# Decode attention over long caches: 4 MB K/V tiles, weight loads in longer runs, and part of the q·k sum on TensorE

## The chip, the cores and the metric

The kernel runs on one core of one Trainium2 chip. The metric is the device time of one execution in microseconds (us); lower is better. A run with rounds executes the changed kernel six times and the kernel before eleven times on the same chip, in turn. A difference of 2% is the line between "same" and "faster" or "slower".

Engine names as in the profile: PE is TensorE (matmul), PEld its weight load, DVE is VectorE, ACT is ScalarE, POOL is GpSimd, SP is SyncE. SPq and ACTq are the sequencers of SyncE and ScalarE, from which the DMAs (loads) of this kernel are issued. Each of them takes its instructions in order: an issue that waits for a buffer holds up every later issue on that sequencer (the run split16_sync below shows it: 35.6 us).

## The reference, cut to what matters

Two independent decode steps, A and B, each with one query token, 32 heads of 128, and a cache of 16,384 rows. B looks only at the last 4,096 rows of its cache. All inputs are bf16.

```python
def _A_ref(x, k_cache, v_cache, wq, wo):        # x (1,1,512), caches (1,32,16384,128)
    q = (x @ wq).reshape(B, Sq, 32, 128).transpose(0, 2, 1, 3)
    scores = jnp.einsum("bhqd,bhkd->bhqk", q, k) * (128 ** -0.5)
    p = softmax(scores, axis=-1)
    o = jnp.einsum("bhqk,bhkd->bhqd", p, v)
    return o.transpose(0, 2, 1, 3).reshape(B, Sq, 32 * 128) @ wo
# _B_ref: the same with k_cache[:, :, Sk - W:, :], v_cache[:, :, Sk - W:, :], W = 4096
# result: concatenate([A, B], axis=-1)
```

Every byte of the caches is used once: 268.4 MB of K and V for A, 67.1 MB for B, 16.8 MB of weights, 352.3 MB in all. The work per byte is small, so this is a problem of loading.

## The kernel before

For each head, K is loaded with 128 partitions of consecutive rows. The score of a row is a multiply on VectorE and a sum over 128 columns, done as a tree of adds on VectorE; the softmax is taken without subtracting a maximum; P·V is one small matmul per row of a partition, accumulated in PSUM. A's head is two units of 64 rows per partition (2 MB of K and 2 MB of V each), B's head is one unit of 32 rows.

```python
    for u in range(NU):                        # A: 2 units of U=64; B: 1 unit of U=32
        kt = kt_pool.tile([P, U, DH], BF16, tag="kt")              # 3 buffers of 2 MB
        nc.sync.dma_start(out=kt[:, :, :], in_=kh[:, u * U : (u + 1) * U, :])
        vt = vt_pool.tile([P, U, DH], BF16, tag="vt")              # 3 buffers of 2 MB
        nc.scalar.dma_start(out=vt[:, :, :], in_=vh[:, u * U : (u + 1) * U, :])
        ...                                    # cut: a GpSimd share that is 0 here
        nc.vector.tensor_tensor(out=prod[...], in0=kt[...], in1=q_broadcast, op=ALU.mult)
        src, width = prod[:, :, :], DH
        while width > 8:                       # 128 -> 64 -> 32 -> 16 -> 8
            dst = tree_pool.tile([P, U, width // 2], BF16, ...)
            nc.vector.tensor_tensor(out=dst, in0=src[left], in1=src[right], op=ALU.add)
            src, width = dst, width // 2
        nc.vector.tensor_reduce(out=sc[:, :], in_=src, axis=X, op=ALU.add)
        nc.scalar.activation(out=p_sb, in_=sc, func=Exp, scale=..., accum_out=colsum)
        for c in range(U):
            nc.tensor.matmul(o_ps[0:1, :], lhsT=p_sb[:, c : c + 1], rhs=vt[:, c, :], ...)
        nc.tensor.matmul(s_ps, lhsT=colsum, rhs=ones_col, ...)
    ...                                        # cut: divide, transpose, multiply by wo
```

K is on the sync queue and V on the scalar queue here already. The weights come in pieces: wq in eight blocks of 512 columns and wo in four blocks of eight heads, for each problem. Each partition's part of such a load consists of runs of 1 KB. q is computed as one row of 512, copied, and spread over 128 partitions by a second matmul.

The softmax here doesn't subtract the row's maximum and nothing guards it: scores larger than these inputs give would overflow.

Of the kernel before, what the change touches and what calls it, by code (L numbers as in the profile page):

```python
# [10 lines left out]
P = 128  # L12
ACT = mybir.ActivationFunctionType
ALU = mybir.AluOpType

HQ, DH = 32, 128


class _ProblemState:
# [3 lines left out]
def _setup_init(nc, st, *, singles):  # L23
    x, wq, wo = st.x, st.wq, st.wo
    D = wq.shape[0]
    st.KC = D // P
    st.NBLK = (HQ * DH) // 512
    xT = singles.tile([P, st.KC], BF16, tag=f"xT{st.name}")
    for c in range(st.KC):
        st.dq.dma_start(  # L30
            out=xT[:, c : c + 1],
            in_=x[0, 0:1, c * P : (c + 1) * P].rearrange("a b -> b a"),
        )
    st.xT = xT
    st.qrow = singles.tile([1, HQ * DH], BF16, tag=f"qrow{st.name}")
    st.qall = singles.tile([P, HQ, DH], BF16, tag=f"qall{st.name}")
    st.wo_view = wo.rearrange("(h p) f -> p h f", p=P)
    st.WOC = 8


def _setup_block(nc, st, j, *, wqb_pool, psq_pool, ones_row):
    KC = st.KC
    wqb = wqb_pool.tile([P, KC, 512], BF16, tag="wqb")
    st.dq.dma_start(
        out=wqb[:, :, :],
        in_=st.wq[:, j * 512 : (j + 1) * 512].rearrange("(c p) f -> p c f", p=P),
    )
    qr_ps = psq_pool.tile([1, 512], F32, tag="qr")
    for kc in range(KC):
        nc.tensor.matmul(  # L50
            qr_ps[0:1, :],
            lhsT=st.xT[:, kc : kc + 1],
            rhs=wqb[:, kc, :],
            start=(kc == 0),
            stop=(kc == KC - 1),
        )
    nc.scalar.copy(st.qrow[0:1, j * 512 : (j + 1) * 512], qr_ps[0:1, :])  # L57
    qbc_ps = psq_pool.tile([P, 4, DH], F32, tag="qbc")
    nc.tensor.matmul(  # L59
        qbc_ps[:, :, :],  # L60
        lhsT=ones_row[0:1, :],
        rhs=st.qrow[0:1, 4 * j * DH : (4 * j + 4) * DH],
        start=True,
        stop=True,
    )
    nc.scalar.copy(st.qall[:, 4 * j : 4 * j + 4, :], qbc_ps[:, :, :])  # L66


def _head(
    nc,  # L70
    st,
    h,
    *,
    small,
    kt_pool,
    vt_pool,
    prod_pool,
    tree_pool,
    wo_pool,
    pso_pool,  # L80
    pss_pool,
    pst_pool,
    ident11,
    ones_col,
):
    U, NU, W = st.U, st.NU, st.W
    inv_sqrt_dh = 1.0 / math.sqrt(DH)

    o_ps = pso_pool.tile([1, DH], F32, tag="o")
    s_ps = pss_pool.tile([1, 1], F32, tag="S")  # L90
    kh = st.k_view[h].rearrange("(p l) d -> p l d", p=P)
    vh = st.v_view[h].rearrange("(p l) d -> p l d", p=P)
    for u in range(NU):
        kt = kt_pool.tile([P, U, DH], BF16, tag="kt")
        nc.sync.dma_start(out=kt[:, :, :], in_=kh[:, u * U : (u + 1) * U, :])
        vt = vt_pool.tile([P, U, DH], BF16, tag="vt")
        nc.scalar.dma_start(out=vt[:, :, :], in_=vh[:, u * U : (u + 1) * U, :])  # L97

        prod = prod_pool.tile([P, U, DH], BF16, tag="prod")
        G = st.G  # L100
        if G > 0:
            nc.gpsimd.tensor_tensor(
                out=prod[:, 0:G, :],
                in0=kt[:, 0:G, :],
                in1=st.qall[:, h : h + 1, :].broadcast_to([P, G, DH]),
                op=ALU.mult,
            )
        nc.vector.tensor_tensor(  # L108
            out=prod[:, G:U, :],
            in0=kt[:, G:U, :],  # L110
            in1=st.qall[:, h : h + 1, :].broadcast_to([P, U - G, DH]),
            op=ALU.mult,
        )
        sc = small.tile([P, U], F32, tag="scores")
        src = prod[:, :, :]
        width = DH
        RT = 8
        while width > RT:
            half = width // 2
            dst = tree_pool.tile([P, U, half], BF16, tag=f"tree{half}")  # L120
            nc.vector.tensor_tensor(  # L121
                out=dst[:, :, :],
                in0=src[:, :, 0:half],
                in1=src[:, :, half:width],
                op=ALU.add,
            )
            src, width = dst[:, :, :], half
        nc.vector.tensor_reduce(  # L128
            out=sc[:, :],
            in_=src,  # L130
            axis=mybir.AxisListType.X,
            op=ALU.add,
        )
        p_sb = small.tile([P, U], BF16, tag="p")
        colsum = small.tile([P, 1], F32, tag="colsum")
        nc.scalar.activation(  # L136
            out=p_sb[:, :],
            in_=sc[:, :],
            func=ACT.Exp,
            scale=inv_sqrt_dh,  # L140
            accum_out=colsum[:, 0:1],
        )
        for c in range(U):
            nc.tensor.matmul(  # L144
                o_ps[0:1, :],
                lhsT=p_sb[:, c : c + 1],
                rhs=vt[:, c, :],
                start=(u == 0 and c == 0),
                stop=(u == NU - 1 and c == U - 1),
            )  # L150
# [155 lines left out]
```

## Time and profile before

Three runs given at first: 863.2, 864.6 and 869.43 us, median 864.6.

| what | before | where it is read |
|---|---|---|
| HBM read | 352.32 MB, 407 GB/s over the span | the page, DMA part |
| load rate from 100 to 800 us | 414 to 424 GB/s | table of stretches |
| VectorE busy | 754.1 us (87%) | the page, busy times |
| TensorE busy | 470.9 us (54%) | the page, busy times |
| packets of 16 KB, 8 KB, 1 KB | 16,427 of 621 ns, 8,210 of 316 ns, 16,384 of 49 ns | packet records of the trace |

These lines of the page of the kernel before give busy times per engine, then rows of 40 slices of the span (each digit is the busy share in tenths; the last row is GB/s).

```profile
span 864.7 us, 12580 instructions
PE 470.9 (54%) x5520; PEld 414.9 (48%) x5520; DVE 754.1 (87%) x707; ACT 73.8 (9%) x291; POOL 0.2 (0%) x4
...
DVE  2699888969898499999989779999999759999995
...
DMA  8999999999999999999999999999999999999992
GB/s 324 413 402 415 415 425 416 421 419 420 420 416 405 426 402 425 418 427 425 425 427 415 416 425 424 416 428 424 426 425 424 409 426 392 403 423 428 426 424 93
```

The DMA row is at 9 nearly everywhere: the kernel is bound by its loads. VectorE is a busy second. Next are the costliest groups of instructions of the same kernel: line, engine, operation, output<-input, count, then busy us and mean ns of one, then the engine's idle time before them and what ended it.

```profile
L108 DVE TENSOR_TENSOR prod<-kt,qall 128x8192 bf16<-128x8192 bf16 (+1 forms) x96 | 355.0, 3698 | 37.9 <-DMA kt<-in_A_k_cache_dram 30.1
L121 DVE TENSOR_TENSOR dst<-dst 128x1024 bf16<-128x1024 bf16 (+3 forms) x288 | 185.9, 657 | 0.1
L121 DVE TENSOR_TENSOR dst<-prod 128x4096 bf16<-128x4096 bf16 (+1 forms) x96 | 184.2, 1918 | 0.0
L128 DVE TENSOR_REDUCE sc<-dst 128x64 f32<-128x512 bf16 (+1 forms) x96 | 55.8, 581 | 0.1
```

The adds of the second line (186 us) are what the change takes off VectorE and gives to TensorE; a reduce like that of the fourth line stays. The table of stretches has, for each, its length, the busy us (and instruction count) of PE, PEld, DVE, ACT and POOL, then the granted TensorE clock, the DMA share and GB/s. These lines are from two such tables of the kernel before:

```profile
100.00:200.00 100.00, 58.34 (x637) 48.61 (x636) 83.66 (x77) 10.82 (x37) 0.00 (x0) 0.73 1.01 419
...
400.00:500.00 100.00, 49.24 (x586) 44.70 (x586) 90.64 (x87) 6.95 (x32) 0.00 (x0) 0.76 1.01 422
...
840.00:848.00 8.00, 0.37 (x3) 0.19 (x3) 8.00 (x9) 0.78 (x3) 0.00 (x0) 0.62 0.67 281
```

In the middle the DMA engines are full. Only at the end (840 to 848 us) are they not, with VectorE busy without a break. There only V's last load is missing. These lines of the timeline are from the end (start us, length us, engine and line, operation, and in brackets how long the engine had stood idle and what released it):

```profile
837.85 1.95 PE L144 MATMUL o_ps<-vt,p_sb 128*1 128x128 bf16 x32 [0.76 <-ACT p_sb L136]
...
847.93 0.26 ACT L136 ACTIVATE p_sb<-sc 128x64 bf16<-128x64 f32 x1 [3.90 <-DVE sc L128]
847.94 0.34 ACTq L97 DMA_DIRECT2D vt<-in_B_v_cache_dram  x1
```

### The profile page before, as it was taken

How to read it: one execution, taken by the hardware profiler on the slowest of the kernel's cores; microseconds unless marked ns; L12 is line 12 of the kernel's file. 1: busy time of each engine (PE TensorE's matmuls, PEld its weight loads, DVE VectorE, ACT ScalarE, POOL GpSimd, SP SyncE). 2: the span in 40 equal slices, each digit the busy share in tenths (PEclk: the TensorE clock that was granted, in tenths of full speed). 3: DMA queues.
4: the chain of work that ended last, by engine and by line, in shares of the span. 5: the costliest groups of instructions: out<-in, count | busy, mean ns of one | idle time of the engine just before them, and what ended most of it. 6: DMA issues, size and time to landing. Idle time of an engine off the chain costs nothing.

```text
span 864.7 us, 12580 instructions
## 1 busy us (share of the span) xinstructions
PE 470.9 (54%) x5520; PEld 414.9 (48%) x5520; DVE 754.1 (87%) x707; ACT 73.8 (9%) x291; POOL 0.2 (0%) x4
## 2 busy tenths in 40 slices
PE   1166764675745364645655256656555345554766
PEld 0055653465634353645655256555555334454665
DVE  2699888969898499999989779999999759999995
ACT  1001111111110011000000000000000000000001
POOL 0000000000000000000000000000000000000000
PEclk9987767768678676788878687687768667687777
DMA  8999999999999999999999999999999999999992
GB/s 324 413 402 415 415 425 416 421 419 420 420 416 405 426 402 425 418 427 425 425 427 415 416 425 424 416 428 424 426 425 424 409 426 392 403 423 428 426 424 93
DMA packets 45625, 353.14 MB, mean 408 GB/s; under 512 B 4609, under 2 KB 20993, under 8 KB 20994
## 3 DMA queue, kind: packets, MB, share of 16 engines
q10 hardware_dynamic: 22784, 176.17, 49.2%
q1 hardware_dynamic: 22786, 176.17, 49.0%
q8 instruction: 43, 0.70, 0.3%
q14 instruction: 12, 0.10, 0.0%
HBM read 352.32 MB, written 0.00 MB: 407 GB/s over the span
## 4 chain that ended last, share of the span: by engine, by line
DVE 44%; DMA 31%; PE 15%; issue 9%; ACTq 0%; ACT 0%; DVEq 0%
DMA vt<-in_A_v_cache_dram 25%; DVE prod L108 24%; DVE dst L121 15%; PE o_ps L144 14%; DVE sc L128 4%; DMA kt<-in_B_k_cache_dram 3%; DMA vt<-in_B_v_cache_dram 2%; PE out_ps L175 1%; DVE ocol L170 0%; DVE recip L159 0%; DMA xT<-in_B_x_dram 0%; ACTq L97 0%; PE ocol_ps L168 0%; ACT orow L161 0%; ACT final_sb L274 0%
## 5 line engine op out<-in xcount | busy, mean ns | idle before, releaser
L144 PE MATMUL o_ps<-vt,p_sb 128*1 128x128 bf16 x5120 | 412.1, 256 | 220.3 <-ACT p_sb L136 130.8
L144 PEld LDWEIGHTS <-p_sb 128*1 128x1 bf16 x5120 | 389.0, 101 | 248.3 <-ACT p_sb L136 185.7
L108 DVE TENSOR_TENSOR prod<-kt,qall 128x8192 bf16<-128x8192 bf16 (+1 forms) x96 | 355.0, 3698 | 37.9 <-DMA kt<-in_A_k_cache_dram 30.1
L121 DVE TENSOR_TENSOR dst<-dst 128x1024 bf16<-128x1024 bf16 (+3 forms) x288 | 185.9, 657 | 0.1
L121 DVE TENSOR_TENSOR dst<-prod 128x4096 bf16<-128x4096 bf16 (+1 forms) x96 | 184.2, 1918 | 0.0
L175 PE MATMUL out_ps<-woc,ocol 128*1 128x512 bf16 x64 | 31.5, 492 | 89.0 <-DVE ocol L170 67.0
L136 ACT ACTIVATE p_sb<-sc 128x64 bf16<-128x64 f32 (+1 forms) x96 | 23.7, 247 | 426.1 <-DVE sc L128 422.5
L128 DVE TENSOR_REDUCE sc<-dst 128x64 f32<-128x512 bf16 (+1 forms) x96 | 55.8, 581 | 0.1
L161 ACT ACTIVATE orow<-o_ps,recip 1x128 bf16<-1x128 f32 x64 | 22.9, 358 | 332.2 <-DVE recip L159 332.2
L159 DVE RECIPROCAL recip<-s_ps 1x1 f32<-1x1 f32 x64 | 9.6, 150 | 47.8 <-PE s_ps L151 47.7
L175 PEld LDWEIGHTS <-ocol 128*1 128x1 bf16 x64 | 5.3, 83 | 85.3 <-DVE ocol L170 78.1
L50 PE MATMUL qr_ps<-wqb,xT 128*1 128x512 bf16 x64 | 20.4, 443 | 27.5 <-DMA wqb<-in_B_wq_dram 15.2
L151 PE MATMUL s_ps<-ones_col,colsum 128*1 128x1 f32 x192 | 18.7, 167 | 28.5 <-DVE recip L159 28.5
L151 PEld LDWEIGHTS s_ps<-ones_col,colsum 128*1 128x1 f32 x192 | 13.7, 87 | 32.4 <-DVE recip L159 31.6
L170 DVE COPY ocol<-ocol_ps 128x1 bf16<-128x1 bf16 x64 | 9.4, 147 | 20.9 <-PE ocol_ps L168 20.9
L168 PEld LDWEIGHTS <-orow 1*128 1x128 bf16 x64 | 6.0, 94 | 40.7 <-ACT orow L161 30.1
L168 PE MATMUL ocol_ps<-ident_94,orow 1*128 1x1 bf16 x64 | 11.2, 175 | 24.5 <-ACT orow L161 24.3
L50 PEld LDWEIGHTS <-xT 128*1 128x1 bf16 x64 | 4.8, 87 | 37.5 <-issue 31.0
L136 ACT ACTIVATION_READ_ACCUMULATOR p_sb<-sc 128x1 f32 x96 | 17.9, 186 | 0.0
L57 ACT CAST qrow<-qr_ps 1x512 bf16<-1x512 f32 x16 | 9.1, 571 | 23.4 <-PE qr_ps L50 23.4
L66 ACT CAST qall<-qbc_ps 128x512 bf16<-128x512 f32 x16 | 9.1, 571 | 1.5 <-PE qbc_ps L59 1.3
L59 PE MATMUL qbc_ps<-qrow,ones_row 1*128 1x512 bf16 x16 | 7.2, 450 | 1.3 <-ACT qrow L57 1.3
(11 smaller groups left out, 4.6 us busy)
## 6 DMA issues: line engine op xcount, KB each, us to landing
vt<-in_A_v_cache_dram ACTq DMA_DIRECT2D x64, 2048.0 KB, 15.9
kt<-in_A_k_cache_dram SPq DMA_DIRECT2D x64, 2048.0 KB, 15.5
kt<-in_B_k_cache_dram SPq DMA_DIRECT2D x32, 1024.0 KB, 14.1
vt<-in_B_v_cache_dram ACTq DMA_DIRECT2D x32, 1024.0 KB, 13.8
wqb<-in_A_wq_dram SPq DMA_DIRECT2D x8, 512.0 KB, 19.1
woc<-in_A_wo_dram SPq DMA_DIRECT2D x4, 1024.0 KB, 22.7
wqb<-in_B_wq_dram ACTq DMA_DIRECT2D x8, 512.0 KB, 22.8
woc<-in_B_wo_dram ACTq DMA_DIRECT2D x4, 1024.0 KB, 24.6
```

The lines of the kernel that those rows point to most:

```text
L50: nc.tensor.matmul(qr_ps[0:1, :], lhsT=st.xT[:, kc : kc + 1], rhs=wqb[:, kc, :], start=(kc == 0), stop=(kc == KC - 1),)
L108: nc.vector.tensor_tensor(out=prod[:, G:U, :], in0=kt[:, G:U, :], in1=st.qall[:, h : h + 1, :].broadcast_to([P, U - G, DH]), op=ALU.mult,)
L121: nc.vector.tensor_tensor(out=dst[:, :, :], in0=src[:, :, 0:half], in1=src[:, :, half:width], op=ALU.add,)
L128: nc.vector.tensor_reduce(out=sc[:, :], in_=src, axis=mybir.AxisListType.X, op=ALU.add,)
L136: nc.scalar.activation(out=p_sb[:, :], in_=sc[:, :], func=ACT.Exp, scale=inv_sqrt_dh, accum_out=colsum[:, 0:1],)
L144: nc.tensor.matmul(o_ps[0:1, :], lhsT=p_sb[:, c : c + 1], rhs=vt[:, c, :], start=(u == 0 and c == 0), stop=(u == NU - 1 and c == U - 1),)
L151: nc.tensor.matmul(s_ps[0:1, 0:1], lhsT=colsum[:, 0:1], rhs=ones_col[:, 0:1], start=(u == 0), stop=(u == NU - 1),)
L159: nc.vector.reciprocal(recip[:, :], s_ps[0:1, 0:1])
L161: nc.scalar.activation(out=orow[:, :], in_=o_ps[0:1, :], func=ACT.Copy, scale=recip[0:1, 0:1],)
L168: nc.tensor.transpose(ocol_ps, orow, ident11)
L170: nc.vector.tensor_copy(ocol[:, :], ocol_ps[:, :])
L175: nc.tensor.matmul(st.out_ps[0:1, :], lhsT=ocol[:, 0:1], rhs=st.woc[:, h % WOC, :], start=(h == 0), stop=(h == HQ - 1),)
```

## The change

The intent is fewer and longer runs for the DMA engines, and less work for VectorE:

- A's K and V are loaded as whole heads: 4 MB tiles, 32 KB runs, two buffers each instead of three of 2 MB.
- B is done in groups of four heads: one 4 MB tile, filled by four 1 MB loads of 8 KB runs.
- wq comes in one load of 4 MB with 32 KB runs (it borrows a V buffer), wo in runs of 4 KB.
- After the multiply and one add on VectorE, eight accumulating matmuls with the identity add the remaining 64 columns to 8 in PSUM, and one VectorE reduce of PSUM finishes the sum.
- x arrives in one DMA, and q is made on all 128 partitions at once, by a matmul with x broadcast over the columns of the stationary operand.
- Smaller parts: B's weights come from the sync queue instead of ScalarE's, the product of the multiply has one buffer instead of two (VectorE alone writes and reads it), and the output rows of four heads are gathered before wo is applied.

```diff
-    for u in range(NU):
-        kt = kt_pool.tile([P, U, DH], BF16, tag="kt")
-        nc.sync.dma_start(out=kt[:, :, :], in_=kh[:, u * U : (u + 1) * U, :])
-        vt = vt_pool.tile([P, U, DH], BF16, tag="vt")
-        nc.scalar.dma_start(out=vt[:, :, :], in_=vh[:, u * U : (u + 1) * U, :])
+    kt = cx.kt_pool.tile([P, L, DH], BF16, tag="kt", name="kt")          # L = 128, whole head
+    nc.sync.dma_start(out=kt[:, :, :], in_=st.k_view[h].rearrange("(p l) d -> p l d", p=P))
+    vt = cx.vt_pool.tile([P, L, DH], BF16, tag="vt", name="vt")
+    nc.scalar.dma_start(out=vt[:, :, :], in_=st.v_view[h].rearrange("(p l) d -> p l d", p=P))
+    for u in range(L // U):
+        p_sb, cs = _scores(nc, cx, kt[:, u * U : (u + 1) * U, :], None, [(0, U, q)])
+        _pv(...)                                                         # 64 matmuls, as before
...                                                  # _scores, after the multiply:
-        while width > RT:
-            dst = tree_pool.tile([P, U, half], BF16, tag=f"tree{half}")
-            nc.vector.tensor_tensor(out=dst, in0=src[left], in1=src[right], op=ALU.add)
-        nc.vector.tensor_reduce(out=sc[:, :], in_=src, axis=X, op=ALU.add)
+    nc.vector.tensor_tensor(out=half, in0=prod[:, :, 0:64], in1=prod[:, :, 64:128], op=ALU.add)
+    red = cx.red_pool.tile([P, U, 8], F32, tag="red", name="red")        # PSUM
+    for b in range(8):
+        nc.tensor.matmul(red, lhsT=cx.ident, rhs=half[:, :, b * 8 : (b + 1) * 8],
+                         start=(b == 0), stop=(b == 7))
+    nc.vector.tensor_reduce(out=sc[:, :], in_=red[:, :, :], axis=AX.X, op=ALU.add)
...
-    wqb_pool, wo blocks of (p h f) order, qrow and qbc matmuls            # 1 KB runs
+    wq_t = cx.vt_pool.tile([P, KC, N], BF16, tag="vt", name="wq_t")
+    nc.sync.dma_start(out=wq_t, in_=st.wq.rearrange("(p c) f -> p c f", c=KC))
+    nc.sync.dma_start(out=st.wo_t, in_=st.wo[8 heads].rearrange("(g p j) f -> p g (j f)", g=2, j=4))
+    nc.tensor.matmul(q_ps[:, :], lhsT=xb[:, c, :], rhs=wq_t[:, c, 512 columns], ...)
...
-    kt_pool = tile_pool(name="kt", bufs=3);  vt_pool = tile_pool(name="vt", bufs=3)
+    cx.kt_pool = pool("kt", 2);  cx.vt_pool = pool("vt", 2)              # of 4 MB each
...
     for h in range(32):
+        if h == G - 1: _weights_q(nc, cx, stB)                           # G = 4
+        _head_A(nc, cx, stA, h)
+        if h % G == G - 1: _group_B(nc, cx, stB, h - G + 1)
-        _head(nc, stA, h);  _head(nc, stB, h)
```

(Several lines are shortened to their core; a "..." marks a cut.)

## The prediction

> **What bounds the kernel now.** The loads. The page shows 352.3 MB read from HBM in 864.7 us (407 GB/s), the DMA row at 9 in nearly every slice, and the two load queues at 98% of the 16 engines' time. The table of stretches gives 414 to 424 GB/s from 100 to 800 us. VectorE is second (754 us, 87%). The chain of waits names VectorE for 44%, DMA for 31%, but those are buffers coming free: a faster VectorE would find the same full DMA engines.
>
> From the packet records: 16,427 packets of 16 KB took 621 ns each, 8,210 of 8 KB 316 ns, 16,384 of 1 KB (all weights) 49 ns: about 10 ns per packet plus 38 per KB. Stretches with K/V alone mostly run at 424 to 429 GB/s, those where a quarter of the bytes are weights near 400. The Trainium skill ("DMA: Bandwidth & Descriptors", Where 436 GB/s comes from) puts the ceiling at 435 GB/s; the best stretches are within 2% of it. 352.3 MB at 435 would be 810 us, an estimated floor.
>
> **What changes.**
> - DMA, on the critical path: 32 KB runs for A's K/V (8,192 packets at an estimated 1,232 ns) save about 5 us; weights in 4 and 32 KB runs (estimated 649 instead of 803 us summed over 16 engines) about 10. B's K/V stays at 8 KB.
> - Start: x in one DMA instead of four, and wq no longer behind it: 2 us earlier. B's wq needs a V buffer and may hold up the sync queue at head 3 for a few us.
> - VectorE, off the path: per 64-row unit it keeps the multiply (4.41 us) and first add (2.27) and swaps the rest (1.2+0.67+0.41+0.67) for one PSUM reduce, estimated at 0.7. 80 units: about 600 us, down from 754.
> - TensorE, off the path: 640 matmuls of 128x512 at 0.22 to 0.44 us, 140 to 280 us more.
> - Buffers: two of 4 MB each instead of three of 2. By durations K is held 13 us, V 25 us after landing, out of 39 us for two heads; K can run ahead of V, so both queues should rarely be empty.
> - Tail: the last loads were starved of buffers from 840 us (245 GB/s to 850), then 12 us of work followed. Afterwards the last group needs 9 us if V lands last, about 20 if K does: perhaps 2 to 7 us worse.
>
> **Sum.** 864.6 - 15 (packets) - 2 (start) - 4 (starved end) + 4 (tail, wq gap) is about 847; I take **846 us**, range **829 to 862** (8 in 10). Faster by over 2% **0.50**, within 2% **0.47**, slower by over 2% **0.03**. Most of the large saving on VectorE should not show.
>
> **What would show it.** Right: no 1 KB packets; 426 to 431 GB/s in the middle; VectorE near 600 us and waiting for K loads; TensorE busier by 140 to 280 us; 10 to 20 us of work after the last load. Wrong: middle stretches under 415 GB/s with both queues waiting for buffers; VectorE waiting long on TensorE's sums.
>
> **What would make it wrong.** Two large buffers may leave both queues empty once per head (slower); TensorE's order may make the next scores wait for V. On the other side, longer runs may get closer to 435 GB/s than fitted, and steadier supply may remove the stretches at 373 to 408 GB/s (faster, to 829).

## The result, and the profile after

| | before | after |
|---|---|---|
| median us, four runs each | 866.08 (863.2 to 869.43) | 856.73 (855.16 to 861.37) |
| ratio, 95% interval | | 0.9888 (0.984 to 0.9935) |

A ratio here, and below, is the mean time of one kernel's runs over the mean of the other's runs of the same rounds, so it is not quite the ratio of the medians that are quoted. The gain is 1.1% and lies within 2%: "same". The prediction had said 846 us, a gain of 2.2%, with "faster by over 2%" as the slightly likelier class. The time lies in its range, which was 33 us wide; about half of the gain that it forecast arrived (9.4 us between the medians, where 864.6 to 846 would be 18.6).

These are the lines of the page after that answer to those shown above.

```profile
span 855.4 us, 13729 instructions
PE 565.1 (66%) x6335; PEld 425.1 (50%) x6336; DVE 590.3 (69%) x346; ACT 64.7 (8%) x275; POOL 0.7 (0%) x6
...
DVE  0469775975783866947967397656969378785791
...
DMA  9999999999999899999999999999999999999992
GB/s 392 423 424 379 420 432 432 426 426 427 434 422 435 334 431 439 424 429 419 433 421 437 423 425 431 427 429 409 419 429 427 434 421 428 432 427 430 401 398 87
```

Two slices stand out against their neighbours at 420 to 439 GB/s: 379 (the fourth, 64 to 86 us) and 334 (the fourteenth, 278 to 299 us). (A packet is counted in the slice where it starts, so that single slices scatter by some GB/s.) Next come the groups after:

```profile
L73 DVE TENSOR_TENSOR prod<-kt,qallA 128x8192 bf16<-128x8192 bf16 x64 | 282.9, 4420 | 90.4 <-DMA kt<-in_A_k_cache_dram 89.5
L90 PE MATMUL red<-half,ident 128*128 128x512 bf16 x640 | 169.0, 403 | 84.5 <-DVE half L80 84.4
L80 DVE TENSOR_TENSOR half<-prod 128x4096 bf16<-128x4096 bf16 x80 | 182.6, 2283 | 0.6
...
L98 DVE TENSOR_REDUCE sc<-red 128x64 f32<-128x512 f32 x80 | 54.1, 680 | 37.0 <-PE red L90 35.6
```

VectorE fell from 754 to 590 us, nearly the 600 that had been forecast, and now waits 89.5 us for K. The Trainium skill ("VectorE: DVE Perf Modes", the perf-mode tier table) gives tensor_reduce one speed for all types, and the traces agree: the reduce of 512 float32 columns of PSUM took 680 ns here, that of 512 bf16 columns of SBUF 668 ns in the run after_tree below. The stretches after:

```profile
100.00:200.00 100.00, 71.91 (x801) 53.16 (x800) 72.11 (x42) 11.40 (x40) 0.00 (x0) 0.88 1.00 427
200.00:300.00 100.00, 62.50 (x684) 45.55 (x683) 71.77 (x40) 5.79 (x29) 0.00 (x0) 0.80 0.97 409
300.00:400.00 100.00, 70.03 (x818) 55.04 (x816) 69.44 (x41) 6.50 (x32) 0.00 (x0) 0.88 1.01 431
```

The rate rose to 427 and 431 GB/s, but from 200 to 300 us it is 409, lower than before (417), at a DMA share of 0.97.

Where did the time go? The trace records each DMA packet with its start, length, size and queue. From these records I split the span of a profiled run into four parts that sum to it: from the start to the first packet of K, V or weights; the time in which such a packet was in flight, summed over the 16 DMA engines and divided by 16 (busy); the engine time without one between the first and the last load packet, likewise divided by 16 (idle); and from the end of the last load packet to the end of the span (tail).

| us | span | start | busy | idle | tail |
|---|---|---|---|---|---|
| before | 864.7 | 4.3 | 838.6 | 9.4 | 12.4 |
| after | 855.4 | 1.8 | 824.9 | 14.4 | 14.3 |
| difference | -9.3 | -2.5 | -13.7 | +5.0 | +1.9 |

The start and the busy time fell about as forecast (-2 and -15). But the loads now stand idle for 5 us more, and the tail is 2 us longer. Each row is one profiled run. A second profile of the changed kernel (after_again, below) has busy 825.9, idle 14.2 and tail 16.0; so a difference of 1 us in busy time or of 2 us in the tail can be chance. The forecast had put these two at zero together (-4 for the starved end, +4 for tail and wq).

Much of the idle time lies in a few places. I looked for stretches with fewer than 11 of the 16 engines loading. Before, there is one of weight, at the end (845.0 to 849.6 us, 3.6 us lost), the "starved end" of the prediction, and a small one at 722.6 (0.7). After, that one has gone, and two new ones are in the middle: 66.0 to 68.5 (2.2 us lost) and 286.2 to 291.5 (3.7); three smaller ones (593, 795, 826 us) lose 1.8 together. One more is at the very end, 838.3 to 841.0 (2.4): all loads had been issued by then, and from 839 to 841 a single packet was in flight at a time, where it is 16 when all engines load. This is the timeline of the kernel after around the larger one: start, length, engine, instruction, and in brackets how long the engine had stood idle and what released it.

```profile
263.78 0.26 ACT L102 ACTIVATE p_sb<-sc 128x64 bf16<-128x64 f32 x1 [0.60 <-DVE sc L98]
...
278.09 4.43 DVE L73 TENSOR_TENSOR prod<-kt,qallA 128x8192 bf16<-128x8192 bf16 x1 [14.29 <-DMA kt<-in_A_k_cache_dram]
282.43 0.68 DVE L98 TENSOR_REDUCE sc<-red 128x64 f32<-128x512 f32 x1
...
285.35 4.42 DVE L73 TENSOR_TENSOR prod<-kt,qallA 128x8192 bf16<-128x8192 bf16 x1
285.37 2.29 PE L90 MATMUL red<-half,ident 128*128 128x512 bf16 x5 [20.01 <-DVE half L80]
...
287.82 2.93 PE L117 MATMUL o_ps<-vt,p_sb 128*1 128x128 bf16 x26
...
289.80 0.33 SPq L195 DMA_DIRECT2D kt<-in_B_k_cache_dram  x1
...
297.71 0.33 ACTq L177 DMA_DIRECT2D vt<-in_A_v_cache_dram  x1
```

The chain of waits of the same kernel, taken of the stretch from 250 to 300 us alone, starts with the load that all of this waits for (start, length, what):

```profile
245.85 32.15 DMA kt<-in_A_k_cache_dram
```

Read it as a ring. VectorE and TensorE each take their instructions in order.

1. The next head's K was issued at 245.85 and, sharing the DMA engines with V and wo, took 32.15 us until all 4 MB had landed.
2. VectorE waited for it 14.29 us. Behind this wait, in its program, stood the last step of the current head's scores: the reduce at 282.43, whose matmuls had ended by 265.4 (TensorE's 20.01 us of idle time before 285.37 say when).
3. The current head's first unit was ready for P·V even then, for ScalarE had made its probabilities at 263.78. But TensorE's program has the sum for the next head's first unit ahead of it, and so it stood idle for 20.01 us until VectorE's add of that unit was done.
4. P·V of both units ran only from 287.82, without a wait for V on its part. V's buffer came free at its end, and the next V was issued at 297.71.
5. The next head's K buffer came free when its second multiply ended (285.35 + 4.42), and the next K load was issued at 289.80.

So the loads that had been issued ran out: by the packet records about 11 engines were at work at 286.2 and none at 289.5. At 66 us it was alike: the next V load was issued at 67.34, the next K load at 67.69, each when its buffer came free.

### The profile page after: what moved, and what is told of

The parts are those of the page before. It is cut to its first block, busy times and chain, and to the rows that moved or that the text cites. A ratio compares the mean times of both kernels' runs of the same rounds, so it can differ in the third digit from the quotient of the medians. Undisturbed runs are those within 1.5% of the kernel's fastest.

```text
span 855.4 us, 13729 instructions
## 1 busy us (share of the span) xinstructions
PE 565.1 (66%) x6335; PEld 425.1 (50%) x6336; DVE 590.3 (69%) x346; ACT 64.7 (8%) x275; POOL 0.7 (0%) x6
## 4 chain that ended last, share of the span: by engine, by line
DMA 55%; DVE 21%; PE 15%; issue 7%; another core or an unknown queue 1%; ACT 1%; ACTq 0%; SPq 0%; DVEq 0%
DMA kt<-in_A_k_cache_dram 26%; DMA vt<-in_A_v_cache_dram 16%; DVE prod L73 12%; PE o_ps L117 10%; DVE half L80 6%; DMA kt<-in_B_k_cache_dram 6%; DMA xTB<-in_B_x_dram 4%; PE red L90 3%; DMA vt<-in_B_v_cache_dram 3%; DVE sc L98 3%; ACT orow L139 0%; PE oc_ps L144 0%; DVE recip L137 0%; PE outB L156 0%
## 5 line engine op out<-in xcount | busy, mean ns | idle before, releaser
L117 PE MATMUL o_ps<-vt,p_sb 128*1 128x128 bf16 x5120 | 351.9, 236 | 112.2 <-DMA vt<-in_A_v_cache_dram 82.6
L117 PEld LDWEIGHTS <-p_sb 128*1 128x1 bf16 x5120 | 333.9, 92 | 132.8 <-issue 112.1
L73 DVE TENSOR_TENSOR prod<-kt,qallA 128x8192 bf16<-128x8192 bf16 x64 | 282.9, 4420 | 90.4 <-DMA kt<-in_A_k_cache_dram 89.5
L90 PE MATMUL red<-half,ident 128*128 128x512 bf16 x640 | 169.0, 403 | 84.5 <-DVE half L80 84.4
L80 DVE TENSOR_TENSOR half<-prod 128x4096 bf16<-128x4096 bf16 x80 | 182.6, 2283 | 0.6
L90 PEld LDWEIGHTS <-ident 128*128 128x128 bf16 x640 | 58.8, 101 | 124.5 <-issue 69.7
L73 DVE TENSOR_TENSOR prod<-kt,qallB 128x4096 bf16<-128x4096 bf16 x32 | 72.0, 2284 | 11.1 <-DMA kt<-in_B_k_cache_dram 9.4
L98 DVE TENSOR_REDUCE sc<-red 128x64 f32<-128x512 f32 x80 | 54.1, 680 | 37.0 <-PE red L90 35.6
L144 PEld LDWEIGHTS <-orow 1*32 1x32 bf16 x256 | 12.2, 111 | 103.6 <-ACT orow L139 60.1
L144 PE MATMUL oc_ps<-one,orow 1*32 1x1 bf16 x256 | 17.4, 171 | 54.1 <-ACT orow L139 53.7
L124 PE MATMUL s_ps<-ones_col,cs 128*1 128x1 f32 x192 | 18.3, 165 | 18.2 <-DVE recip L137 17.6
L124 PEld LDWEIGHTS s_ps<-ones_col,cs 128*1 128x1 f32 x192 | 11.4, 84 | 31.5 <-DVE recip L137 19.7
L156 PE MATMUL outA<-wo_t,oc 128*1 128x512 bf16 x32 | 12.3, 528 | 4.9 <-DVE oc L153 4.9
L45 PEld LDWEIGHTS <-xbA 128*128 128x128 bf16 x32 | 3.7, 116 | 18.6 <-DVE xbA L40 13.6
## 6 DMA issues: line engine op xcount, KB each, us to landing
wo_t<-in_A_wo_dram SPq DMA_DIRECT2D x4, 1024.0 KB, 21.2
```

Source lines behind the costliest of these rows:

```text
L45: nc.tensor.matmul(q_ps[:, :], lhsT=xb[:, c, :], rhs=wq_t[:, c, j * 512 : (j + 1) * 512], start=(c == 0), stop=(c == KC - 1),)
L73: nc.vector.tensor_tensor(out=prod[:, k0 : k0 + n, :], in0=kv[:, k0 : k0 + n, :], in1=q.rearrange("p (o d) -> p o d", o=1).broadcast_to([P ...
L80: nc.vector.tensor_tensor(out=half[:, :, :], in0=prod[:, :, 0 : DH // 2], in1=prod[:, :, DH // 2 : DH], op=ALU.add,)
L90: nc.tensor.matmul(red[:, :, :], lhsT=cx.ident[:, :], rhs=half[:, :, b * W : (b + 1) * W], start=(b == 0), stop=(b == nb - 1),)
L98: nc.vector.tensor_reduce(out=sc[:, :], in_=red[:, :, :], axis=AX.X, op=ALU.add)
L124: nc.tensor.matmul(s_ps[0:1, 0:1], lhsT=cs, rhs=cx.ones_col[:, 0:1], start=first, stop=last,)
```

## The experiments

In the 18 kernels below, "after" stands for the changed kernel and "split16" for the first repair of it. The expectations name some theories by a letter; where a letter is not spelled out there, it stands for what follows. P: long runs make the packets cheaper, and this is what the change gains. L: it matters that a tile of 4 MB lands and comes free as a whole, so that the engines wait for the second half before they may start on the first. G: the size of a buffer is what counts, two of 4 MB against four of 2 MB. K and V: one of the two loads alone makes the gaps. T: the sum on TensorE costs time at the end. S: the slack that it gives VectorE is needed once the tiles are large. E: the order of the last groups makes the tail. R: VectorE is held up by small steps that wait for TensorE (reciprocal, row cast). Q: TensorE's program order makes the tail. I: V's loads are held up because ScalarE issues them between its other work.

All outputs are right. This table has all results; the last four columns are the split of the profiled run, as above. Most were profiled within 1.6 us of their median; after_tree 3.4 us above it (its slowest execution), split16_sync 2.2 us below, split16_tree_free 10 us below.

| run | median us | ratio to before (95%) | start | busy | idle | tail |
|---|---|---|---|---|---|---|
| after_again | 859.04 | 0.9896 (0.9852 to 0.9940) | 1.8 | 825.9 | 14.2 | 16.0 |
| split16 | 855.02 | 0.9845 (0.9806 to 0.9885) | 1.9 | 828.6 | 7.1 | 15.5 |
| tiles2mb | 860.54 | 0.9912 (0.9875 to 0.9948) | 1.8 | 827.9 | 7.9 | 20.7 |
| w1k | 868.85 | 1.0004 (0.9967 to 1.0041) | 2.2 | 833.7 | 17.2 | 14.9 |
| splitk | 858.36 | 0.9899 (0.9869 to 0.9929) | 1.8 | 826.5 | 10.0 | 17.3 |
| splitv | 855.54 | 0.9861 (0.9827 to 0.9894) | 2.0 | 826.4 | 9.3 | 16.4 |
| wqfirst | 855.21 | 0.9863 (0.9834 to 0.9893) | 1.8 | 824.6 | 11.9 | 15.6 |
| before_pesum | 874.27 | 1.0085 (1.0053 to 1.0117) | 4.4 | 837.9 | 9.8 | 19.0 |
| after_tree | 857.00 | 0.9903 (0.9872 to 0.9934) | 1.8 | 826.1 | 19.2 | 11.6 |
| split16_tree | 861.48 | 0.9950 (0.9920 to 0.9980) | 1.8 | 828.6 | 10.5 | 18.3 |
| alast | 857.50 | 0.9900 (0.9870 to 0.9930) | 1.8 | 828.3 | 8.1 | 18.7 |
| alast_tree | 862.05 | 0.9949 (0.9916 to 0.9981) | 1.8 | 828.4 | 10.5 | 21.2 |
| after_free | 860.18 | 0.9917 (0.9883 to 0.9950) | 1.8 | 827.2 | 13.9 | 15.1 |
| split16_free | 857.29 | 0.9887 (0.9849 to 0.9925) | 1.9 | 830.3 | 7.0 | 16.7 |
| split16_tree_free | 870.24 | 1.0010 (0.9964 to 1.0056) | 1.8 | 831.5 | 9.0 | 16.2 |
| alast_tree_free | 873.73 | 1.0067 (1.0032 to 1.0102) | 1.8 | 831.8 | 27.4 | 11.4 |
| split16_sync | 890.66 | 1.0266 (1.0223 to 1.0308) | 2.0 | 833.6 | 24.5 | 26.8 |
| split16_ahead | 855.54 | 0.9857 (0.9826 to 0.9888) | 1.8 | 827.8 | 7.9 | 15.5 |

### First call: packets or landing? (after_again, split16, tiles2mb, w1k)

after_again is the changed kernel once more, without an edit, as the yardstick.

> The changed kernel, unaltered, as the control of this call. About 857 us (855 to 861), 0.985 to 0.993 of the kernel before. Theory G (buffers): the idle of the 16 DMA engines between the first and the last load comes to 6 to 9 us again, at nearly the same places (near 66 and 286 us), because the order of each engine's instructions is fixed. Theory N (noise): the gaps lie elsewhere or are gone.

It measured 859.04 us (855.68 to 864.17), with gaps at the same places: 66.2 us (2.5 lost), 286.9 (2.6) and 796 to 800 (2.1). So the gaps belong to the program and not to one run.

split16 keeps everything of the change but loads A's tiles in two halves. A unit can start when its half has landed; the runs are 16 KB again. The buffers stay two of 4 MB.

```diff
-    nc.sync.dma_start(out=kt[:, :, :], in_=st.k_view[h].rearrange("(p l) d -> p l d", p=P))
-    nc.scalar.dma_start(out=vt[:, :, :], in_=st.v_view[h].rearrange("(p l) d -> p l d", p=P))
+    for u in range(L // U):
+        nc.sync.dma_start(out=kt[:, u * U : (u + 1) * U, :], in_=kh[:, u * U : (u + 1) * U, :])
+        nc.scalar.dma_start(out=vt[:, u * U : (u + 1) * U, :], in_=vh[:, u * U : (u + 1) * U, :])
```

> A's 4 MB K and V tiles are filled by two DMAs of 2 MB each, so 16 KB runs as before the change; buffers and everything else as after. Theory P (time of the packets adds up on the 16 engines): 16,384 packets at 621 ns instead of 8,192 at 1,224 ns are 157 us of engine time, 10 us slower than after, about 867 us. Theory L (landing): the first half of a tile can be worked on 5 to 10 us earlier, K buffers come free earlier, the gaps near 286 us and some of the tail go: at most 3 us slower than after, or faster.

It measured 855.02 us; all six runs (854.61 to 855.48) lie below the fastest of after_again (855.68). Busy time rose by 2.7 us, idle time fell by 7.1. So the long runs of A's K and V save about 3 us of packet time, and landing as a whole costs more than that. The stretches around the gap show it, first in the kernel after, then in split16 (the last two numbers are DMA share and GB/s):

```profile
276.00:284.00 8.00, 0.00 (x0) 0.00 (x0) 5.91 (x3) 0.35 (x2) 0.00 (x0) 0.50 1.01 434
284.00:292.00 8.00, 6.63 (x48) 4.16 (x48) 7.97 (x4) 0.00 (x0) 0.00 (x0) 0.55 0.47 179
292.00:300.00 8.00, 7.94 (x144) 7.74 (x141) 4.53 (x2) 0.36 (x1) 0.00 (x0) 1.00 1.02 421
```

```profile
276.00:284.00 8.00, 5.51 (x22) 2.17 (x23) 5.00 (x4) 0.36 (x1) 0.00 (x0) 0.79 1.00 419
284.00:292.00 8.00, 3.42 (x9) 1.01 (x7) 5.23 (x4) 0.70 (x4) 0.00 (x0) 0.79 1.02 431
292.00:300.00 8.00, 7.49 (x131) 7.17 (x130) 3.55 (x1) 0.00 (x0) 0.00 (x0) 1.00 0.99 418
```

In split16 no gap is left before 829 us; one at 829.5 to 834.1 loses 2.3 (see the fifth call). VectorE's longest wait for a K of A falls from 14.3 to 9.6 us.

tiles2mb makes the buffers themselves small: A's tiles are 2 MB again (four buffers of K, four of V), B goes in pairs of heads, and wq takes two buffers. Everything else is the change.

```diff
+        kt = cx.kt_pool.tile([P, U, DH], BF16, tag="kt", name="kt")       # in the loop over units
+        nc.sync.dma_start(out=kt[:, :, :], in_=kh[:, u * U : (u + 1) * U, :])
-    cx.kt_pool = pool("kt", 2)
-    cx.vt_pool = pool("vt", 2)
+    cx.kt_pool = pool("kt", 4)
+    cx.vt_pool = pool("vt", 4)
```

> Four K and four V buffers of 2 MB instead of two of 4 MB, the same bytes of SBUF; 16 KB runs for A's K/V and wq. Theory G (the idle DMA time after the change comes from giving back buffers 4 MB at a time): idle between first and last load falls from 8 to under 3 us and the tail after the last load from 15.5 to about 12 us, so 8 to 9 us faster than split16, within 3 us of after. Rival (gaps come from the order of TensorE's work or from wq of B, whatever the tile size): within 3 us of split16, gaps as in after.

The idle time fell to 7.9 us, about as in split16, so giving buffers back in halves adds nothing to landing in halves. But the tail grew to 20.7 us, and the time is 860.54, no better than after_again and 5.5 us slower than split16. Theory G had the fall of the idle time about right (6.3 us against after_again), but split16 has it too with 4 MB buffers; the time was missed because of the tail, and why the tail grew is not shown.

w1k keeps the change but brings the weights in runs of 1 KB again (wq in eight column blocks, wo in four).

```diff
-    nc.sync.dma_start(out=wq_t[:, :, :], in_=st.wq.rearrange("(p c) f -> p c f", c=KC))
+    for j in range(N // 512):
+        nc.sync.dma_start(out=wq_t[:, :, j * 512 : (j + 1) * 512], in_=wq_v[:, :, j * 512 : (j + 1) * 512])
```

> The changed kernel with its weights alone in 1 KB runs again (same tiles, same buffers, one DMA per 512 columns). Theory P: 16,384 packets at 49 ns instead of 256 at 1,224 and 2,048 at 162 ns are 159 us of engine time: 10 us slower than after, about 867 us. Rival (the weights' short runs cost little, the gain of the change came from elsewhere): within 3 us of after.

It measured 868.85 us, 9.8 us above after_again: the whole gain of the change has gone. Its 16,386 packets of 1 KB (two of them are the stores of the result) took 49.9 ns each. Busy time rose by 7.8 us, idle by 3.0. The weights, a twentieth of the bytes, account for about the whole net gain of the change.

### Second call: which load, wq, and the sum alone (splitk, splitv, wqfirst, before_pesum)

splitk loads only K in halves, splitv only V.

```diff
-    nc.sync.dma_start(out=kt[:, :, :], in_=...)          # splitk; splitv: the scalar line of vt
+    for u in range(L // U):
+        nc.sync.dma_start(out=kt[:, u * U : (u + 1) * U, :], in_=kh[:, u * U : (u + 1) * U, :])
```

> The changed kernel with only A's K tiles filled by two DMAs of 2 MB (16 KB runs); V whole. Theory K (the gaps come from K: scores of a head can start only when all 4 MB of K have landed, the K buffer comes back late, and TensorE, which has the next head's score sums ahead of this head's P.V in its program, gives V back late too): the gaps in the middle go as in split16, under 1.5 us in all, about 855 us. Rival V (whole V tiles are what holds up the queues): gaps of 5 us or more stay, about 859 us.

> The changed kernel with only A's V tiles filled by two DMAs of 2 MB; K whole. Theory K: gaps of 5 us or more stay near 66 and 286 us, 858 to 861 us. Rival V: gaps go, about 855 us.

Neither came out as a theory of K alone or V alone had it. The gap at 66 has gone in both, and that at 286 is 0.6 us or nothing; but each has a late gap, splitk 3.4 us at 819 to 826, splitv 3.4 at 789 to 796. Only with both halves is the middle free of gaps. By time splitv (855.54) is as good as split16, splitk (858.36) is not. Their profiled runs differ by less (spans 854.0 and 855.6), and this is idle time (9.3 and 10.0) and tail (16.4 and 17.3); the rest of the 2.8 us between the medians stays open.

wqfirst loads B's wq at the start instead of at head 3, to see whether the gap at 66 us comes from wq holding a V buffer.

```diff
     _weights_q(nc, cx, stA)
+    _weights_q(nc, cx, stB)
     for h in range(stA.H):
-        if h == G - 1:
-            _weights_q(nc, cx, stB)
```

> The changed kernel with B's wq and q worked out at the very start, before A's head 0. Theory W (the gap at 66 us is B's wq waiting for a V buffer and holding up the sync queue): that gap of 2.2 to 2.5 us goes and the time falls by about as much, to 856 us or so; the gap near 286 us stays. Rival: the gap at 66 us is the first K buffers coming back late (head 0's scores start only at 34 us) and stays, or moves, with no gain over 1 us.

The gap at 66 did not go: it moved to 75.8 to 78.5 and kept its size (2.4 us). That at 286 went, others came (387 us, 1.0 lost; 791 us, 2.5 lost). The time, 855.21, was 3.8 us below after_again, though that was another chip. By ratio (0.9863 against 0.9896, and 0.9845 for split16) the intervals overlap; moving one load may thus be worth nearly as much as the halves, and why is not shown. So the place of a gap depends on where in the sequence the wq load stands, but the wq load is not its cause; the prediction's "wq gap" was not what lies at 66 us.

before_pesum is the kernel before with only the sum changed: one add on VectorE, eight identity matmuls, one PSUM reduce.

```diff
-        while width > RT:                     # tree of four adds on VectorE
-            ...
+        nc.vector.tensor_tensor(out=half, in0=prod[:, :, 0:64], in1=prod[:, :, 64:128], op=ALU.add)
+        red = st.red_pool.tile([P, U, WR], F32, ...)                     # PSUM
+        for b in range(nb):
+            nc.tensor.matmul(red, lhsT=st.ident, rhs=half[:, :, b * WR : (b + 1) * WR], ...)
```

> The kernel before with one part of the change alone: after the first add, 512 elements per 64 rows are summed on TensorE (8 identity matmuls, 4 for B) and one reduce from PSUM; loads, tiles and weights as before. Theory D (the loads bound it, VectorE's time is off the path): VectorE busy falls from 754 to about 600 us and the time changes by less than 4 us (862 to 868), the most it can win being the 3.6 us of DMA idle at 845 us. Rival (the chain of waits, with 44% VectorE, is to be believed): faster by 10 us or more.

VectorE's busy time fell to 607.9 us, and the kernel became 0.85% slower: 874.27 us, all six runs (872.93 to 876.02) above the kernel before's highest of this call (871.45). Busy and idle time of the loads did not move; the tail grew from 12.4 to 19.0 us. The timeline of its end shows one reason. (Here the sum also shares the two PSUM buffers of q's projection; the profile names 12.3 us of waits of q's matmuls for the reduce, and no run separates these.)

```profile
851.88 4.15 PE L149 MATMUL o_ps<-vt,p_sb 128*1 128x128 bf16 x59
855.87 0.19 PE L156 MATMUL s_ps<-ones_col,colsum 128*1 128x1 f32 x2
855.99 1.68 PE L126 MATMUL red<-half,ident 128*128 128x512 bf16 x7
857.78 0.69 DVE L133 TENSOR_REDUCE sc<-red 128x64 f32<-128x512 f32 x1 [6.55 <-PE red L126]
```

The score sum of a late unit stands in TensorE's queue behind the P·V of the unit before it (851.88 to 855.99), and VectorE waits 6.55 us. On VectorE the same sum waited for nobody.

### Third call: is VectorE's relief needed at all? (after_tree, split16_tree, alast, alast_tree)

after_tree is the change with the sum back on VectorE; split16_tree is the same on split16.

```diff
-    half = cx.half_pool.tile(...); nc.vector.tensor_tensor(out=half, ...)
-    for b in range(nb): nc.tensor.matmul(red, lhsT=cx.ident, rhs=half[...], ...)
-    nc.vector.tensor_reduce(out=sc[:, :], in_=red[:, :, :], axis=AX.X, op=ALU.add)
+    while width > 8:
+        nc.vector.tensor_tensor(out=dst, in0=src[:, :, 0:hw], in1=src[:, :, hw:width], op=ALU.add)
+    nc.vector.tensor_reduce(out=sc[:, :], in_=src, axis=AX.X, op=ALU.add)
```

> The changed kernel with the sum on VectorE as before the change (adds down to 8 columns, one reduce), TensorE's identity matmuls gone. Theory T (the sum on TensorE costs at the end: the last scores wait there behind the P.V matmuls of the head before): tail after the last load from 15.5 to about 12 us, time about 855 us, 3 to 4 us faster than after. Rival S (with 4 MB tiles VectorE's slack is needed to give K buffers back in time): VectorE busy near 755 us, more idle DMA time in the middle, slower than after by 3 us or more.

> split16 (A's 4 MB tiles filled in two halves) with the sum on VectorE. Theory T: tail from 14.4 to about 11 us and no new gaps, since the halves land early enough: about 852 us, 3 us faster than split16. Rival S: slower than split16 by 3 us or more, gaps of several us back.

In after_tree both theories show and cancel: the tail is 11.6 us, shorter by 4.4 than after_again's, and the idle time 19.2, longer by 5.0. The time is the same (ratios 0.9903 and 0.9896). The split is of after_tree's slowest execution, so its sizes are rough. On split16 the relief is worth 6.5 us (861.48 against 855.02, on the same chip; ratios 0.9950 and 0.9845): with the tree the idle time rises by 3.4 us and the tail by 2.8. That the tail rose too, where in after_tree it fell, was against T.

alast (built on split16) puts B's last group before A's last four heads, so that the end is one head and not four.

```diff
-        if h % G == G - 1:
+        if h % G == G - 1 and h < stA.H - 1:
+        if h == stA.H - G - 1:
+            _group_B(nc, cx, stB, stA.H - G)
+            _store(nc, cx, stB, out, stA.DN)
```

> split16 with B's last group worked before A's last four heads, so that the last loads are the halves of one A head instead of four B heads. Theory E (the tail is the last group's serial end: four heads' P.V and finish after the last load, 2.4 us each): tail from 14.4 to 8 or 10 us, about 850 us. Rival: the tail is the last scores' path through VectorE and TensorE, whatever the heads, and stays above 13 us; no gain.

> alast with the sum on VectorE. If T and E both hold and add: tail 7 to 8 us, about 848 us, 2% under the kernel before. If only E holds: as alast. If S holds: slower than alast.

E was a miss: the tail grew, from 15.5 to 18.7 us (alast against split16) and to 21.2 with the tree. In alast the last reduce of scores waits 7.68 us for TensorE's sum, which stands behind P·V. These two have a flaw as well: the store of B's row is now issued on the sync queue ahead of A's last K loads. It cost little here but a lot in the next call.

### Fourth call: small steps taken off VectorE (after_free, split16_free, split16_tree_free, alast_tree_free)

The reciprocal is done as a power of -1 on GpSimd and the cast on ScalarE, so that VectorE never waits for P·V. The same edit was put on after, split16, split16_tree and alast_tree.

```diff
-    nc.vector.reciprocal(recip[:, :], s_ps[0:1, 0:1])
+    nc.scalar.copy(s_sb[:, :], s_ps[0:1, 0:1])
+    nc.gpsimd.tensor_tensor(out=recip[:, :], in0=s_sb[:, :], in1=cx.minus[:, :], op=ALU.pow)
-        nc.vector.tensor_copy(oc[:, :], st.oc_ps[:, :])
+        nc.scalar.copy(oc[:, :], st.oc_ps[:, :])
```

> The changed kernel with the reciprocal on GpSimd (s to the minus one, s copied from PSUM by ScalarE) and the cast of the head outputs on ScalarE, so VectorE never waits for P.V itself. Theory R (VectorE's in-order wait in the reciprocal delays the next scores): idle plus tail from 29 to 22 us or less, about 850 us. Theory Q (the sum on TensorE behind P.V delays them): within 2 us of after, 856 to 859 us.

> split16 with the reciprocal and cast off VectorE. R: tail from 15.5 to 11 us or less, about 850 us. Q: within 2 us of split16, 854 to 857 us, VectorE's waits of several us now at the PSUM reduce.

> split16 with the sum on VectorE and the reciprocal and cast off it: scores depend on K alone. If R or Q is the cause: K's scores run ahead, the tail is P.V and finish after the last V, 10 us or less, against 18 in split16_tree; about 850 us, 10 us faster than split16_tree. If VectorE's own 755 us are the limit with these loads: about 860 us as split16_tree.

> alast_tree with the reciprocal and cast off VectorE: scores depend on K alone and only half a head's P.V follows the last load. R or Q: tail 8 to 9 us against 21 in alast_tree, about 847 us, which would be 2% under the kernel before. Otherwise about 860 us.

R found no support. after_free (860.18) is level with the change, split16_free (857.29) no better than split16. The waits only moved: in after_free VectorE waits 103.6 us in its PSUM reduces for TensorE's sums, against 35.6 in the kernel after. The two runs with the tree are worse and blurred. split16_tree_free has one run at 860.27 and five at 869 to 871, and its profile was of a run of the first kind, so its split does not explain its median; I don't know why it has two levels. In alast_tree_free the loads stood still for 16 us (799.6 to 816.2), because the sync queue waited 46.6 us for B's row, which the store needs, and A's last K loads stood behind it. That run says nothing about R or Q. It does show what a 1x1 operation on GpSimd can take beside VectorE (timeline):

```profile
805.05 6.86 POOL L130 TENSOR_TENSOR recip<-s_sb,minus 1x1 f32<-1x1 f32 x1 [3.48 <-ACT s_sb L129]
```

The shortest of these took 0.54 us in after_free, the longest 9.77 us in split16_tree_free. The Trainium skill ("SBUF — State Buffer", Who interferes with whom) says that GpSimd shares a pair of ports with VectorE under an exclusive lock. The times agree with it: the mean was 1.76 us in after_free and 4.26 us in split16_tree_free, where VectorE adds more. No run here separates the lock from other causes.

### Fifth call: the queues and TensorE's order (split16_sync, split16_ahead)

split16_sync issues V from the sync queue as well.

```diff
-        nc.scalar.dma_start(out=vt[:, u * U : (u + 1) * U, :], in_=vh[:, u * U : (u + 1) * U, :])
+        nc.sync.dma_start(out=vt[:, u * U : (u + 1) * U, :], in_=vh[:, u * U : (u + 1) * U, :])
```

> split16 with all K and V loads on the sync queue, none on ScalarE's. Theory I (in split16 the last 1 MB of V was issued at 833 us, behind a wait of ScalarE for the reciprocal): idle between loads from 7 to 4 us, tail no longer, about 851 us. Rival (one queue in order makes K wait behind V's buffers, and K can no longer run ahead): idle grows, slower than split16, 857 us or more.

The cure failed, strongly: 890.66 us, 35.6 us above split16 (another chip; 35.1 above split16_ahead on the same one), the only "slower". Idle time rose from 7.1 to 24.5 us and the tail from 15.5 to 26.8. The waits of the sync queue (what was waited for: us in total, times, longest us):

```profile
SPq L180 <- PE s_ps L124: 300.6, 30, 14.1
SPq L179 <- DVE prod L73: 226.4, 25, 15.6
```

L180 is V's issue, waiting until P·V has given a V buffer back. While it waits, the next K load stands behind it, although K's buffer may be free. The Trainium skill ("DMA: Bandwidth & Descriptors", Issuing engines are not separate DMA queues) says that issuing from several engines saves only the sequencer's time. The busy time of the loads is indeed nearly the same (833.6 against 828.6 us); the section leaves out what most of these 35.6 us show, that each sequencer waits in order. The run is no clean test of theory I, for it also put V in line with K; the next one tells more.

split16_ahead emits a unit's P·V after the next unit's scores, so that in TensorE's queue the sums no longer stand behind P·V.

```diff
-        _pv(nc, cx, acc, p_sb[:, :], vt[:, u * U : (u + 1) * U, :], cs[:, 0:1], ...)
-    _finish_head(nc, cx, st, h, acc)
+        _flush(cx)                            # runs the P·V of the unit before
+        cx.job = job                          # this unit's _pv (and _finish_head), for later
```

> split16 with each unit's P.V emitted after the next unit's scores, so that TensorE's and VectorE's programs have the next scores first. Theory Q: the last scores no longer wait behind the P.V of head 31; tail from 15.5 to 12 us or less, about 851 us. Rival: V buffers come back one unit later, idle grows by as much or more; 855 us or slower.

Nothing changed: 855.54 us, idle 7.9, tail 15.5. Q is not confirmed by this; it is not excluded either, since at the end one reduce still waits 2.99 us for a sum.

But this run speaks against theory I. First V's last issues in split16, then the last one in split16_ahead:

```profile
833.07 0.36 ACT L139 ACTIVATE orow<-o_ps,recip 1x128 bf16<-1x128 f32 x1 [10.58 <-DVE recip L137]
833.08 0.33 ACTq L198 DMA_DIRECT2D vt<-in_B_v_cache_dram  x1
```

```profile
823.33 0.45 ACTq L212 DMA_DIRECT2D vt<-in_B_v_cache_dram  x1
```

In split16 the last 1 MB of V did stand behind ScalarE's work, as theory I has it, and it was issued 9.75 us later than in split16_ahead. Yet the last load packet ended at 837.5 us in both. What is late is something else: in split16_ahead, with every load issued, the packet records show about 8 packets in flight at a time from 833.5 to 837 us, where it is 16 when all engines load. So about half of the engines had finished their share while the other half had not. The gap of split16 at 829.5 to 834.1 shows the same 8. What makes the shares end unevenly was not tested.

### What the tail consists of

In the kernel after, V's last loads were issued at 829.34. The timeline of its end:

```profile
840.02 0.69 DVE L98 TENSOR_REDUCE sc<-red 128x64 f32<-128x512 f32 x1 [1.03 <-PE red L90]
...
843.49 0.15 DVE L137 RECIPROCAL recip<-s_ps 1x1 f32<-1x1 f32 x1 [2.71 <-PE s_ps L124]
...
845.84 0.15 DVE L137 RECIPROCAL recip<-s_ps 1x1 f32<-1x1 f32 x1 [2.19 <-PE s_ps L124]
...
850.54 0.15 DVE L137 RECIPROCAL recip<-s_ps 1x1 f32<-1x1 f32 x1 [2.20 <-PE s_ps L124]
...
852.75 0.57 ACT L218 CAST rowB<-outB 1x512 bf16<-1x512 f32 x1 [1.66 <-PE outB L156]
```

After the last scores come four heads one behind the other, about 2.35 us from reciprocal to reciprocal, and then the row, its cast and its store. Changes of order (alast), of the small steps (the free runs) and of TensorE's queue (split16_ahead) did not make the time shorter; where the tail alone was shorter (11.6 in after_tree, 11.4 in alast_tree_free), the loads had stood idle for longer before (19.2 and 27.4). What sets the 14 to 16 us stays open.

## Why the prediction was right or wrong

Right:

- **The bound.** "The loads": the DMA share stayed near 1 after the change, and what the change gained is packet time and start.
- **The start.** "2 us earlier": 2.5 us.
- **The packets.** "About 15" us in sum: busy time fell by 13.7. The weights' share, forecast as about 10, was 7.8 of busy time in w1k (9.8 of time, with the idle time that came too). The share of A's K and V, forecast as about 5, was nearer 3 (2.7 of busy time in split16). The ceiling in the prediction, 435 GB/s after the Trainium skill ("DMA: Bandwidth & Descriptors", Where 436 GB/s comes from), agrees with the best stretches of 10 us with K/V alone after the change, 427 to 432 GB/s.
- **VectorE.** "About 600 us": 590.3. It waits for K loads, as said, and "most of the large saving on VectorE should not show" held: with the kernel before's tiles the same sum on TensorE alone made things worse (before_pesum, +0.85%), with the change's tiles it is worth nothing measurable (after_tree). Only with the half loads is it worth 6.5 us.
- **The tail, by luck.** "2 to 7 us worse": 1.9 in the pair of profiles, 3.6 in after_again, against the kernel before. But the forecast lay between two cases, "9 us if V lands last, about 20 if K does". V landed last (its last loads were issued at 829.34, K's by 804.3), and the tail was 14.3 to 16.0 us, not 9.

Wrong:

- **The step that failed is the one of the buffers**: "K can run ahead of V, so both queues should rarely be empty", and with it the idle terms in the sum, "- 4 (starved end) + 4 (tail, wq gap)". The starved end was indeed removed (3.6 us lost before, by issue order on ScalarE and not for want of a buffer, as shown above), though 2.4 us were lost at the new end. But idle time in all rose by 5.0 us instead of falling, and with the tail's 1.9 the two terms came to +6.9 us instead of 0. That is nearly all of the difference between the sum of the prediction and the result: with -13.7 for -15 (+1.3) and -2.5 for -2 (-0.5) it makes 7.7 us, and 864.7 - 15 - 2 - 4 + 4 = 847.7 against 855.4 measured in the profiled run is 7.7.
- The reason why that step failed: I had counted how long a buffer is held after it lands, and compared this with the period of two heads. I had not counted the time in which a full buffer can't be used because an engine, in its program order, waits for another buffer's load. In the trace a full V buffer stayed held while VectorE waited 14.29 us for all of the next K, and TensorE 20.01 us behind it. split16 removed the gaps in the middle and 7.1 us of idle time by halving the loads alone; this part is shown. The prediction's own sign for being wrong, a middle stretch under 415 GB/s, came in one of seven (409 from 200 to 300 us). That the ring of waits at 286 us is what happens at the other gaps is read from the trace at one place in full and at a second in part (66 us), and not tested one by one. Why splitk and splitv each leave one late gap stays open.
- The listed risks named it: "two large buffers may leave both queues empty", "TensorE's order may make the next scores wait for V". The first came true in a few places rather than once per head; the second came the other way round, P·V waiting in TensorE's queue behind the next scores. Both were given too little weight in the middle of the range.
- **The wq gap** was placed wrongly: the gap at 66 us moved with wq but did not vanish (wqfirst).
- **TensorE**: "busier by 140 to 280 us". The new matmuls took 169.0 us, in the range, but TensorE as a whole rose by only 94, mainly because P·V took 351.9 us instead of 412.1. The mean granted clock rose from 0.761 to 0.842 between the two profiles; no run isolates what this did. It did not matter for the time.
- **The class.** With these terms at their measured sizes the change lies at 1.1%, and none of the 18 runs came 2% below the kernel before. The best is split16, 1.55% below it; a version that wins by more was not found.

## What to carry to other kernels

When the loads are the bound, count packets first: here a twentieth of the bytes, put back into runs of 1 KB, cost about as much time (9.8 us) as the whole change had gained. A larger load is not free even into the same buffers: ask what each engine, in its own order, waits for while that tile lands, and which full buffers are stuck behind that wait; loading a large tile in halves keeps its buffers and most of the gain. An engine that has been relieved off the critical path gains nothing until another change makes its slack needed, and the engine that takes the work over can put it at the back of its own queue at the end.

## What the Trainium skill lacked or had wrong

- "DMA: Bandwidth & Descriptors", Issuing engines are not separate DMA queues: it says that several issuing engines save only sequencer time. With K and V issued from one engine the kernel took 35.6 us longer (890.66 against 855.02), and the sync queue's waits (300.6 us before V's issues, 226.4 before K's) show that an issue that waits for its buffer holds up those behind it. The section lacks a sentence on waits in order.
- "DMA: Bandwidth & Descriptors", Specifications: it gives 512 B as the least transfer for the line rate. Here packets took 49 ns at 1 KB, 161.6 at 4 KB, 316 at 8 KB, 618 to 621 at 16 KB (split16 and before) and 1,224 at 32 KB, about 10 ns plus 38 ns per KB, so 1 KB runs move bytes at 0.78 of the rate of 32 KB runs (38.2 ns per KB over 49), and w1k cost 9.8 us. A table of load rates by length of run, for this chip, is lacking.
- "DMA: Bandwidth & Descriptors", Where 436 GB/s comes from: it says that for loads from HBM the limit of about 358 GB/s binds. A core alone read at 424 to 432 GB/s here, as the page "HBM Reference" (Specifications) says of a core alone (about 425); the first sentence holds for pairs of cores only, or is not shown here.
- "DMA: Bandwidth & Descriptors", the rules: it advises large loads of 1 MB and more. It has nothing on too large: 4 MB loads against two of 2 MB each into the same buffers cost 4.0 us (after_again against split16).
- "SBUF — State Buffer", Who interferes with whom: it has the lock, and ratios for who is slowed, but no times for a small GpSimd operation. Here one on one element took from 0.54 to 9.77 us beside VectorE's work (split16_tree_free); that the lock does this is not shown.
